# Attention beside a Fourier mixing layer on one core: the main loop's order of work from a written list instead of three round patterns

## The chip, the core and the metric

The kernel runs on one core of one Trainium2 chip. Its engines work side by side, each through its own queue in order: TensorE (PE, with its weight loads as PEld) multiplies, VectorE (DVE), ScalarE (ACT) and GpSimd (POOL) work on elements, and SyncE (SP) issues the DMA transfers. Matmul results go to PSUM, which has eight banks here named S0 to S5, F0 and V. The metric is the device time of one execution in microseconds: before the change 1810.23 us (median of three, 1810.04 to 1810.98).

## The reference

S is 2048, D 640, H 32 heads of width 20, one key and value head shared by all.

```python
g = sigmoid((x * gate_w).sum(-1, keepdims=True))
# Fourier mixing
a_ = einsum("bsd,ed->bse", x, dft_hid_re); b_ = einsum("bsd,ed->bse", x, dft_hid_im)
a = einsum("ts,bse->bte", dft_seq_re, a_) - einsum("ts,bse->bte", dft_seq_im, b_)
# attention, one k and v for 32 heads
q = x @ wq; k = x @ wk; v = x @ wv
p = softmax(q k^T * 20 ** -0.5); b = (p @ v) @ wo
out = g * a + (1 - g) * b
```

## The kernel before, in words

A first stage makes q, k and v, a second one the two products with the hidden DFT (tiles `ab`, line 125, with the first scores of head pair 0 among them). Then comes the main loop, 240 rounds, which this change rewrites; 16 rounds of another pattern (`ROUND_LAST`) for the last head pair; and the product with `wo`.

Three streams of matmuls are interleaved on PE in the main loop, by an order that the kernel writes out by hand (`manual_schedule`):

- **y**, the DFT along the sequence (line 645), done as seven block products. A y matmul has 64 rows: the contraction is halved between rows 0 to 63 (group 0, `y0`) and rows 64 to 127 (group 1, `y1`), and both halves add into the same bank F0. 96 y matmuls make one group of outputs, 48 groups fall in the main loop. The left operand is loaded and split in two by POOL (`load_c`, `split_c`, lines 450, 454, 455, tiles `craw`, `ch`, `cl`), in half blocks of 24 y matmuls per row group and with three buffers; the right operand by `split_x` (lines 482, 485, 486).
- **scores.** Two heads make a pair; head 0 has its queries and keys in rows 0 to 63, head 1 in rows 64 to 127. A score is computed twice. As `a` (line 330, queries by keys) it is read by DVE (line 337), which takes the row maximum; `a_reduce` and `a_final` turn a whole pair's maxima into two more rows of the queries' buffer, through DRAM. As `b` (line 750, keys by queries, with the maximum subtracted by those two rows) it is read by ACT (line 759), which writes the exponentials to one of 16 buffers `pt`. The a stream runs ahead of the b stream by a whole pair and `LEAD` = 12 units of a head. a and b share the six banks S0 to S5, so a score has to wait until the reader of its bank's previous score is done.
- **V**, the product of the exponentials with v (line 763, `av_step`): 128 rows by 32 columns, four column groups side by side, two passes of float32, so eight matmul instructions make one step.

A matmul of 64 rows in group 0 runs beside one in group 1. So the order pairs y of one row group with scores of the other, and changes sides: since both halves of y add into one bank, a y matmul that starts on a new side waits for the first reader (of an a or b) that was issued after the last y of the old side (`Halves.run`, `Halves.scored`). ROUND_10 and ROUND_9 are used in the ratio 3 to 2; in both a half round is y0 with the scores of rows 64 to 127, then a V, and the other half is y1 with the scores of rows 0 to 63, then a V. `c` is a `b` that takes the newest free `pt` buffer, `E` is the eviction of a finished y group by ACT.

The queries of a pair stand in one of three buffers; `load_qs` fills the next one by six DMAs on SP's queue when the a stream has done 17 units of a pair. `later(n, f)` runs `f` after n ticks, and a tick is every second `a` of the main loop. All loads of the main loop are issued from SP's one queue.

Of the kernel before, what the change touches and what calls it, by code (L numbers as in the profile page):

```python
# [10 lines left out]
AF = mybir.ActivationFunctionType  # L11
# [7 lines left out]
S = 2048  # L19
# [4 lines left out]
NT = S // P  # L24
NPAIR = H // 2
LAST = NPAIR - 1
# [8 lines left out]
def kernel(  # L35
# [274 lines left out]
    def load_qs(p):  # L310
        t = qbuf[p % 3]
        qs[p] = t
        for hh in range(2):
            r = slice((2 * p + hh) * DH, (2 * p + hh + 1) * DH)
            b = 64 * hh
            move(t[b : b + 20], qh_d[r])
            move(t[b + 20 : b + 40], qh_d[r])
            move(t[b + 40 : b + 60], ql_d[r])
# [47 lines left out]
    def later(n, f, *args):  # L366
        todo.append((clock["n"] + n, f, args))
# [6 lines left out]
            f(*args)  # L374

    NA = NPAIR * 64
    state = [0, 0]

    def a_half(hh, tag="A", main=False):
        u = state[hh]  # L380
        if u >= NA:
            return
        ins = a_unit(u, hh, tag)
        if main:
            halves.scored(ins)
        state[hh] = u + 1
        if state[1 - hh] <= u:
            return
        if u % 64 == 16 and u // 64 + 1 < NPAIR:
            load_qs(u // 64 + 1)  # L390
        if u % 64 == 63:
            later(1, a_reduce, u // 64)
            later(3, a_final, u // 64)


    cpools = [ctx.enter_context(tc.tile_pool(name="cp0", bufs=1))]
# [99 lines left out]

    load_qs(0)
    rot = Rot(["B", "F", "B", "F"])
    LEAD = 12
    done = 0  # L500
    for t in range(NT):
        load_x2(t + 2)
# [124 lines left out]
    class Halves:  # L627
# [3 lines left out]
            self.todo = [[], []]  # L631
            self.last = self.mark = None

        def put(self, ps2, w, x, start, stop):

            one = len(ps2) == 1
            for g, r in enumerate(RG):
                s0, s1 = start and not (one and g == 1), stop and not (one and g == 0)
                self.todo[g].append((ps2, w[r], x[r], s0, s1))

        def run(self, g):
            while not self.todo[g]:
                next(ys)
            ps, w, x, start, stop = self.todo[g].pop(0)
            mm = nc.tensor.matmul(ps[g % len(ps)], w, x, start=start, stop=stop)  # L645
            if len(ps) == 1:

                if not start and self.last != g:
                    tc.add_manual_dep(mm.ins, self.mark.ins.name, ORDER, reason="turns with a bank")
                self.last, self.mark = g, None  # L650

        def scored(self, ins):
            if self.mark is None:
                self.mark = ins

    ORDER = mybir.DependencyInfo(mybir.DependencyClass.Sync, mybir.DependencyReason.DATA)
    halves = Halves()
# [21 lines left out]
    def y_in(n, k):  # L679

        got = []
        for q, (_, old, _) in enumerate(PRODUCTS[n][2]):
            if old is not None:
                t = op.tile([P, HALF], F32, tag=f"ya{q}", name="ya")
                move(t, y_block(old, k))
                got.append(t)
        return got
# [15 lines left out]
    def f_stream():  # L703

        load_c(0, 1)
        split_c(0, 1)  # L710
        for g, (n, k) in enumerate(GROUPS):
            ps = [bank("F0", f"y_{n}_{k}")[:, :HALF]]
            if g >= GMAIN:
                ps.append(bank("S5", f"y_{n}_{k}_1")[:, :HALF])
            y0 = y_in(n, k)
            for sh in range(2):
                h, l = c_ops.pop((g, sh))
                load_c(g + 1, sh)
                for j in range(SJ):
                    if j == SJ // 2:  # L720
                        split_c(g + 1, sh)
                        if sh == 0:
                            load_x(n + 1, k)
                        else:
                            split_x(n + 1, k)
                    jj = sh * SJ + j
                    x = x_ops[n, jj // 2]
                    hi, lo = x[:, jj % 2], x[:, 2 + jj % 2]
                    last = jj == NT - 1
                    halves.put(ps, h[:, j], hi, jj == 0, False)  # L730
                    halves.put(ps, h[:, j], lo, False, False)
                    halves.put(ps, l[:, j], hi, False, last)
                    if last:
                        ended.append({"n": n, "k": k, "ps": ps, "y": y0})
                    yield

# [5 lines left out]

    ptfree = list(range(16))

    def b_unit(p, hh, kc, qc, tag, newest):
        b = 64 * hh
        ps = bank(tag, f"b_{p}_{kc}_{qc}_{hh}")
        nc.tensor.matmul(  # L750
            ps,
            ks[b : b + 62, kc * P : (kc + 1) * P],
            qs[p][b : b + 62, qc * ROW : (qc + 1) * ROW],
            start=True,
            stop=True,
        )
        slot = ptfree.pop(-1 if newest else 0)
        t = pp.tile([P, ROW], F32, tag=f"pt{slot}", name="pt")
        halves.scored(nc.scalar.activation(t, ps, AF.Exp, scale=SCALE))  # L759
        pt[(hh, kc, qc)] = t, slot  # L760

    def av_mm(ps, g, t, kc, first, last):
        nc.tensor.matmul(ps[32 * g : 32 * g + 32, :], vsb[:, kc, :], t, start=first, stop=last)  # L763

    def av_step(p, qh, kc):
        if kc == 0:
            av[qh] = bank("V", f"av_{p}_{qh}")
        for hh in range(2):
            for j in range(2):
                t, slot = pt.pop((hh, kc, 2 * qh + j))  # L770
                av_mm(av[qh], 2 * hh + j, t, kc, kc == 0, kc == NT - 1)
                ptfree.append(slot)

    def finish_half(p, qh):
        ob = op.tile([P, ROW], F32, name="ob")
        nc.scalar.activation(ob, av[qh], AF.Copy)
        for hh in range(2):
            h = 2 * p + hh
            for j in range(2):
                js = slice((2 * qh + j) * ROW, (2 * qh + j + 1) * ROW)  # L780
                g = 32 * (2 * hh + j)
                move(sum_d[h : h + 1, js], ob[g + DH : g + DH + 1])
                move(oT_d[h * DH : (h + 1) * DH, js], ob[g : g + DH])
        if p == LAST:
            sm = op.tile([P, 16], F32, name="sm")
            ts = slice(qh * S // 2, (qh + 1) * S // 2)
            for hh in range(2):
                move(sm[64 * hh : 64 * hh + 64], sum_d[2 * p + hh, ts].rearrange("(s t) -> s t", t=16))
            later(4, finish_last, ts, sm)
        elif qh == 1:  # L790
            sm = op.tile([P, 32], F32, name="sm")
            move(sm, sum_d[2 * p : 2 * p + 2].rearrange("h (s t) -> (h s) t", t=32))
            later(24, finish_sums, p, sm)
# [11 lines left out]
    def finish_last(ts, sm):  # L805
# [10 lines left out]

    ROUND_10 = (
        "a1S0 y0 b1S3 y0 y0 c1S1 y0 y0 a1S2 y0 a1S5 y0 y0 a1S4 y0 b1S0 c0S3 V a0S1 y1 y1 b0S0 "  # L820
        "y1 y1 a0S5 y1 a0S3 y1 y1 b0S2 y1 y1 a0S4 y1 c0S0 c1S1 V y0"
    ).split()
    ROUND_9 = (
        "a1S2 y0 b1S0 y0 y0 a1S1 y0 a1S5 y0 y0 a1S4 y0 y0 b1S3 y0 c0S2 c1S0 V a0S5 y1 b0S2 y1 "
        "y1 a0S1 y1 c0S0 y1 y1 a0S3 y1 y1 a0S4 y1 E0 b1S2 c0S5 V"
    ).split()

    ROUND_LAST = (
# [3 lines left out]
    ).split()  # L832
    ROUNDS = [(p, qh, kk) for p in range(NPAIR) for qh in range(2) for kk in range(NT // 2)]

    BEFORE = {
        4: (lambda: load_wo(range(3)), lambda: load_o(0), lambda: load_o(1)),
# [1 line left out]
        6: (lambda: split_o(0), lambda: load_o(2)),  # L838
        7: (lambda: [load_y(tb) for tb in range(4)],),
    }  # L840
    old = []
    for rnd in ROUNDS:
        p, qh, kk = rnd
        nb, na = [0, 0], 0
        turn = (p * NT + qh * SJ + kk) % 5
        new = [(p, qh, 2 * kk), (p, qh, 2 * kk + 1)]
        for what in ROUND_LAST if p == LAST else ROUND_10 if turn < 3 else ROUND_9:
            if what == "V":
                if old:
                    st = old.pop(0)  # L850
                    av_step(*st)
                    if st[2] == NT - 1:
                        finish_half(*st[:2])
                continue
            g = int(what[1])
            if what[0] == "y":
                halves.run(g)
            elif what[0] == "E":
                if p == LAST or turn == 4:
                    y_evict()  # L860
            elif what[0] in "bc":
                b_unit(p, g, 2 * kk + nb[g] // 2, 2 * qh + nb[g] % 2, what[2:], what[0] == "c")
                if p == LAST and sum(nb) % 2 == 0:
                    tick()
                nb[g] += 1
            else:
                if na % 2 == 0:
                    tick()
                a_half(g, what[2:], True)
                na += 1  # L870
        old += new
        if p == LAST and qh == 1:
            for f in BEFORE.get(kk, ()):
                f()
    for _ in range(2):
        y_evict()
    split_o(1)
# [69 lines left out]
```

## Time and profile before

| what | us |
|---|---|
| median of three runs | 1810.23 |
| profiled execution, first to last instruction | 1807.7 |
| PE busy | 1799.4 |
| DVE busy | 1457.3 |
| ACT busy | 1243.2 |
| POOL busy | 822.1 |
| granted TensorE clock | 1.000 |

The profiled execution's span is 2.5 us under the median. The stages by the trace: up to 89 us the projections, up to 248 us the hidden DFT, from 248 to 1626 us the main loop, to 1732 us the last pair's rounds, and then the output product. PE's busy share says that there is always a matmul under way, not that both row groups are: that is read from the starts of single matmuls.

### The profile page before, as it was taken

Reading aid. Unit: us, or ns where it says so; the run is one execution under the profiler, and the core shown is the slowest. Engines: PE = TensorE matmul, PEld = TensorE weight load, DVE = VectorE, ACT = ScalarE, POOL = GpSimd, SP = SyncE. Lnnn points to the kernel's source line nnn. Section 1 sums busy time; section 2 is a strip of 40 time slices with the busy share of each in tenths; the row PEclk is TensorE's granted clock in tenths of the full one; section 3 lists DMA queues with packets and bytes.
Section 4 is the critical chain, followed back from the end, with each engine's and each line's share of the span. In section 5 each row is a group of like instructions: output and inputs, shape, how many; then the busy total and the mean of one; then the engine's idle time right before and its main releaser. Section 6 shows DMA issues by size and latency. Waiting matters only on the chain.

```text
span 1807.7 us, 40911 instructions
## 1 busy us (share of the span) xinstructions
PE 1799.4 (100%) x16342; PEld 1215.1 (67%) x16342; DVE 1457.3 (81%) x2335; ACT 1243.2 (69%) x2327; POOL 822.1 (45%) x559
## 2 busy tenths in 40 slices
PE   9999999999999999999999999999999999999999
PEld 7799976666666666666666666666666666657789
DVE  4469988888888888888888888888888888853354
ACT  5432247777777777777777777777777777776731
POOL 1012136444546464666655565565554444342241
PEclk9999999999999999999999999999999999999999
DMA  8763334332344433444353434353433342315666
GB/s 267 227 192 99 115 100 139 116 108 84 130 125 133 121 119 106 153 126 152 112 167 101 156 112 141 113 153 115 136 112 114 87 126 79 97 59 169 207 215 209
DMA packets 131003, 243.89 MB, mean 135 GB/s; under 512 B 26356, under 2 KB 77556, under 8 KB 128292
## 3 DMA queue, kind: packets, MB, share of 16 engines
q1 hardware_dynamic: 130012, 238.00, 41.8%
q0 software_dynamic: 800, 3.28, 0.6%
q8 instruction: 128, 2.10, 0.5%
q14 instruction: 63, 0.52, 0.1%
HBM read 194.62 MB, written 50.86 MB: 136 GB/s over the span
## 4 chain that ended last, share of the span: by engine, by line
PE 99%; DMA 0%; POOL 0%; ACT 0%; DVE 0%; issue 0%; SPq 0%; ACTq 0%
PE av L763 28%; PE y L645 20%; PE a L330 18%; PE b L750 15%; PE ab L125 8%; PE q L114 1%; PE o L114 1%; PE q L115 1%; PE q L116 1%; PE o L116 1%; PE o L115 1%; PE kv L210 0%; PE kv L211 0%; DMA xr<-in_xT_dram 0%; DMA xr<-x_d 0%; ACT pt L759 0%
## 5 line engine op out<-in xcount | busy, mean ns | idle before, releaser
L337 DVE TENSOR_REDUCE mx<-a 128x1 f32<-128x512 f32 x2048 | 1291.3, 684 | 170.0 <-PE a L330 164.6
L759 ACT ACTIVATE pt<-b 128x512 f32<-128x512 f32 x2048 | 1110.7, 597 | 334.9 <-PE b L750 289.9
L645 PE MATMUL y<-x,ch 64*128 64x320 f32 x3584 | 796.6, 317 | 1.1 <-ACT pt L759 1.1
L330 PE MATMUL a<-ks,qs 60*128 60x512 f32 x2048 | 740.0, 416 | 0.0
L645 PEld LDWEIGHTS y<-x,ch 64*128 64x128 f32 x3584 | 552.3, 184 | 85.5 <-ACT pt L759 83.5
L750 PE MATMUL b<-qs,ks 62*128 62x512 f32 x2048 | 596.5, 405 | 0.6 <-DVE mx L337 0.6
L330 PEld LDWEIGHTS a<-ks,qs 60*128 60x128 f32 x2048 | 379.8, 185 | 277.0 <-ACT pt L759 197.4
L763 PE MATMUL av<-pt,vsb 128*32 128x512 f32 x4096 | 542.0, 604 | 0.0
L645 PE MATMUL y<-x,cl 64*128 64x320 f32 x1792 | 528.3, 311 | 0.5 <-POOL cl L455 0.5
L645 PEld LDWEIGHTS y<-x,cl 64*128 64x128 f32 x1792 | 314.7, 184 | 42.0 <-ACT pt L759 41.1
L750 PEld LDWEIGHTS b<-qs,ks 62*128 62x128 f32 x2048 | 314.0, 185 | 23.4 <-issue 6.7
L450 POOL TENSOR_TENSOR craw<-craw 128x1024 f32<-128x1024 f32 x80 | 191.1, 2388 | 236.2 <-DMA craw<-in_cre_dram 88.8
L455 POOL TENSOR_TENSOR cl<-craw,ch 128x1024 fp32r<-128x1024 f32 x98 | 234.2, 2389 | 7.9
L454 POOL CAST ch<-craw 128x1024 fp32r<-128x1024 f32 x98 | 101.7, 1038 | 182.2 <-PE y L645 153.4
L763 PEld LDWEIGHTS av<-pt,vsb 128*32 128x32 f32 x4096 | 82.3, 108 | 139.8 <-issue 131.5
L125 PE MATMUL ab<-wh,xh 64*128 64x320 f32 x640 | 136.0, 307 | 0.0
L125 PE MATMUL ab<-wl,xh 64*128 64x320 f32 x640 | 135.8, 306 | 0.0
L125 PE MATMUL ab<-wh,xl 64*128 64x320 f32 x640 | 135.6, 305 | 0.0
L698 POOL TENSOR_TENSOR ya<-yt,ya 128x320 f32<-128x320 f32 x64 | 59.4, 944 | 142.8 <-ACT yt L671 142.2
L524 ACT ACTIVATE half<-ab 128x320 f32<-128x320 f32 x64 | 28.0, 438 | 114.1 <-PE ab L125 100.8
L125 PEld LDWEIGHTS ab<-wh,xl 64*128 64x128 f32 x640 | 98.7, 184 | 0.0
L125 PEld LDWEIGHTS ab<-wl,xh 64*128 64x128 f32 x640 | 98.6, 185 | 0.0
(88 smaller groups left out, 1082.7 us busy)
## 6 DMA issues: line engine op xcount, KB each, us to landing
craw<-in_cre_dram SPq DMA_DIRECT2D x96, 512.0 KB
craw<-in_cim_dram SPq DMA_DIRECT2D x96, 512.0 KB
xr<-x_d SPq DMA_DIRECT2D x88, 320.0 KB
qs<-qh_d SPq DMA_DIRECT2D x64, 160.0 KB
x_d<-both SPq DMA_DIRECT2D x64, 160.0 KB
ya<-y_d SPq DMA_DIRECT2D x64, 160.0 KB
y_d<-ya SPq DMA_DIRECT2D x64, 160.0 KB
xr<-in_xT_dram SPq DMA_DIRECT2D x20, 256.0 KB
```

The lines of the kernel that those rows point to most:

```text
L114: nc.tensor.matmul(ps, wh, xh, start=(i == 0), stop=False)
L125: nc.tensor.matmul(ps, w[r], x[r], start=(i == 0 and k == 0), stop=(i == n - 1 and k == 2))
L330: nc.tensor.matmul(ps, qs[p][b : b + 60, qb * P : (qb + 1) * P], ks[b : b + 60, c * ROW : (c + 1) * ROW], start=True, stop=True,)
L337: return nc.vector.tensor_reduce(mx[p][:, hh, qb, c : c + 1], ps, axis=AX.X, op=ALU.max)
L450: eng.tensor_tensor(raw, raw, raws[1], op=PRODUCTS[n][0][1])
L454: eng.tensor_copy(h, raw)
L455: eng.tensor_tensor(l, raw, h.bitcast(F32), op=ALU.subtract)
L645: mm = nc.tensor.matmul(ps[g % len(ps)], w, x, start=start, stop=stop)
L698: nc.gpsimd.tensor_tensor(ya, yt, ya, op=how)
L750: nc.tensor.matmul(ps, ks[b : b + 62, kc * P : (kc + 1) * P], qs[p][b : b + 62, qc * ROW : (qc + 1) * ROW], start=True, stop=True,)
L759: halves.scored(nc.scalar.activation(t, ps, AF.Exp, scale=SCALE))
L763: nc.tensor.matmul(ps[32 * g : 32 * g + 32, :], vsb[:, kc, :], t, start=first, stop=last)
```

## The change

The two patterns ROUND_10 and ROUND_9 go. In their place stands a list of 8942 letters (`PLAN`) for all 240 rounds, one letter for each piece of work: `0` and `1` are a y matmul of row group 0 or 1, `V` a step with v, `-` an eviction of a y group, and the 24 letters of `SCORES` a score: `a` to `f` and `A` to `F` an `a` of head 0 or 1, `g` to `l` and `G` to `L` a `b` of head 0 or 1, the letter's place naming its bank S0 to S5. The list holds 2304 each of `0` and `1`, 944 `a` and 960 `b` for each head, 478 `V` and 48 `-`. Beside that:

- `put` no longer fixes which y matmul starts or stops a bank: `run` counts them (`grp`), so that either side can begin.
- The `pt` buffer of a `b` is chosen by `pick`: the newest of those whose last reader is known to be done from waits made before; `known`, `last` and `waits` keep that account while the program is built.
- `LEAD` is 16 instead of 12, so eight more `a` fall into the second stage.
- `load_qs` of the next pair is called only when both heads have issued all `b` that use its buffer (`need`, `ready`).
- `a_final` comes two ticks after a pair's last `a` instead of three.
- The last pair's 16 rounds keep their pattern; a step with v still comes two steps behind its scores (`LAG`).

```diff
+    taken = {"b": [0, 0], "a": 0, "V": 0}
+    need = []
+    def ready():
+        while need and min(taken["b"]) >= 64 * (need[0] - 2):
+            load_qs(need.pop(0))
...
-            load_qs(u // 64 + 1)
+            need.append(u // 64 + 1)
+            ready()
         if u % 64 == 63:
             later(1, a_reduce, u // 64)
-            later(3, a_final, u // 64)
+            later(2, a_final, u // 64)
...
-    LEAD = 12
+    LEAD = 16
...
+            one = len(ps) == 1
+            k = 0 if one else g
+            start, stop = grp[k] == 0, grp[k] == (6 if one else 3) * NT - 1
+            grp[k] += 1
             mm = nc.tensor.matmul(ps[g % len(ps)], w, x, start=start, stop=stop)
...
+    def pick(own):
+        lim = max(own, known["ACT"])
+        fit = [s for s in ptfree if s[0] <= lim]
+        best = max(fit or ptfree)
+        known["ACT"] = max(known["ACT"], best[0]) if not fit else known["ACT"]
+        ptfree.remove(best)
+        return best[1]
...
-    ROUND_10 = (
-        "a1S0 y0 b1S3 y0 y0 c1S1 y0 y0 a1S2 y0 a1S5 y0 y0 a1S4 y0 b1S0 c0S3 V a0S1 y1 y1 b0S0 "
-        "y1 y1 a0S5 y1 a0S3 y1 y1 b0S2 y1 y1 a0S4 y1 c0S0 c1S1 V y0"
-    ).split()
...
+    SCORES = "abcdefABCDEFghijklGHIJKL"
+    PLAN = (
+        "gBId1K11l1a111h1c11j11k11f11ah11i11j11eFVHa0E0I000F00J0H000A0C00K0DL00H0A00K0VCd0L0A0hEV1i1lDh11aVeI"
+        "0L0D00A0H000I0K00F0D00H00A0C000F000K0BjVVa11k1c11j11f1h11a1k11c11j1h11f11e1g1-VVJcHfGe1VJc1h11f1g111"
...
+    for what in PLAN:
+        if what == "V":
+            next_v()
+        elif what == "-":
+            y_evict()
+            known["y"] = taken["b"][0] + taken["b"][1] - 1
+        elif what in "01":
+            halves.run(int(what))
+        else:
+            kind, s = divmod(SCORES.index(what), 6)
+            if kind >= 2:
+                if min(state) >= NA and sum(taken["b"]) % 2 == 0:
+                    tick()
+                next_b(kind - 2, f"S{s}")
+            else:
+                if taken["a"] % 2 == 0:
+                    tick()
+                waits(f"S{s}", -1)
+                a_half(kind, f"S{s}", True)
+                taken["a"] += 1
```

More of the change, by code (lines that the diff above doesn't have):

```diff
@@ L632, in __init__, with put @@
             self.last = self.mark = None
-        def put(self, ps2, w, x, start, stop):
-            one = len(ps2) == 1
+        def put(self, ps2, w, x, grp):
             for g, r in enumerate(RG):
-                s0, s1 = start and not (one and g == 1), stop and not (one and g == 0)
-                self.todo[g].append((ps2, w[r], x[r], s0, s1))
+                self.todo[g].append((ps2, w[r], x[r], grp))
         def run(self, g):
@@ L643, in run, with scored @@
                 next(ys)
-            ps, w, x, start, stop = self.todo[g].pop(0)
+            ps, w, x, grp = self.todo[g].pop(0)
+            one = len(ps) == 1
+            k = 0 if one else g
+            start, stop = grp[k] == 0, grp[k] == (6 if one else 3) * NT - 1
+            grp[k] += 1
             mm = nc.tensor.matmul(ps[g % len(ps)], w, x, start=start, stop=stop)
-            if len(ps) == 1:
+            if one:
                 if not start and self.last != g:
                     tc.add_manual_dep(mm.ins, self.mark.ins.name, ORDER, reason="turns with a bank")
+                    known["PE"] = max(known["PE"], self.exp)
+                if start:
+                    known["PE"] = max(known["PE"], known["y"])
                 self.last, self.mark = g, None
-        def scored(self, ins):
+        def scored(self, ins, n=-1):
             if self.mark is None:
-                self.mark = ins
+                self.mark, self.exp = ins, n
     ORDER = mybir.DependencyInfo(mybir.DependencyClass.Sync, mybir.DependencyReason.DATA)
@@ L715, in f_stream @@
             y0 = y_in(n, k)
+            grp = [0, 0]
             for sh in range(2):
@@ L728, in f_stream @@
                     hi, lo = x[:, jj % 2], x[:, 2 + jj % 2]
[L729 to L733, printed above, removed]
+                    halves.put(ps, h[:, j], hi, grp)
+                    halves.put(ps, h[:, j], lo, grp)
+                    halves.put(ps, l[:, j], hi, grp)
+                    if jj == NT - 1:
                         ended.append({"n": n, "k": k, "ps": ps, "y": y0})
@@ L741, with waits, b_unit @@
     pt = {}
-    ptfree = list(range(16))
-    def b_unit(p, hh, kc, qc, tag, newest):
+    ptfree = [(-1, k) for k in range(16)]
+    known = {"PE": -1, "ACT": -1, "y": -1}
+    last = {}
+    def waits(tag, n):
+        own = last.get(tag, -1)
+        last[tag] = n
+        if own <= known["PE"]:
+            return -1
+        known["PE"] = own
+        return own
+    def pick(own):
[5 more added lines that the diff above has]
+        return best[1]
+    def b_unit(p, hh, kc, qc, tag):
         b = 64 * hh
@@ L756, in b_unit @@
         )
-        slot = ptfree.pop(-1 if newest else 0)
+        n = taken["b"][0] + taken["b"][1]
+        slot = pick(waits(tag, n))
         t = pp.tile([P, ROW], F32, tag=f"pt{slot}", name="pt")
-        halves.scored(nc.scalar.activation(t, ps, AF.Exp, scale=SCALE))
-        pt[(hh, kc, qc)] = t, slot
+        halves.scored(nc.scalar.activation(t, ps, AF.Exp, scale=SCALE), n)
+        pt[(hh, kc, qc)] = t, (n, slot)
     def av_mm(ps, g, t, kc, first, last):
@@ L770, in av_step @@
                 t, slot = pt.pop((hh, kc, 2 * qh + j))
+                known["PE"] = max(known["PE"], slot[0])
                 av_mm(av[qh], 2 * hh + j, t, kc, kc == 0, kc == NT - 1)
@@ L812, in finish_last @@
             move(rx_d[h * DH : (h + 1) * DH, ts], rec_d[h : h + 1, ts].to_broadcast([DH, S // 2]))
-    ROUND_10 = (
-        "a1S0 y0 b1S3 y0 y0 c1S1 y0 y0 a1S2 y0 a1S5 y0 y0 a1S4 y0 b1S0 c0S3 V a0S1 y1 y1 b0S0 "
-        "y1 y1 a0S5 y1 a0S3 y1 y1 b0S2 y1 y1 a0S4 y1 c0S0 c1S1 V y0"
-    ).split()
[L823 to L826, printed above, removed]
+    SCORES = "abcdefABCDEFghijklGHIJKL"
@@ L832 @@
     ).split()
-    ROUNDS = [(p, qh, kk) for p in range(NPAIR) for qh in range(2) for kk in range(NT // 2)]
+    STEPS = [(p, qh, kc) for p in range(NPAIR) for qh in range(2) for kc in range(NT)]
     BEFORE = {
@@ L840 @@
     }
[L841 to L847, printed above, removed]
-            if what == "V":
[L849 to L857, printed above, removed]
-            elif what[0] == "E":
[L859 to L863, printed above, removed]
-                    tick()
[L865 to L874, printed above, removed]
@@ new lines, with next_b, next_v @@
+    LAG = 2
+    taken["V"] = LAG
+    def next_b(g, tag):
+        r, nb = divmod(taken["b"][g], 4)
+        p, qh, kc = STEPS[2 * r + nb // 2]
+        b_unit(p, g, kc, 2 * qh + nb % 2, tag)
+        taken["b"][g] += 1
+        ready()
+    def next_v():
+        st = taken["V"] - LAG
+        taken["V"] += 1
+        if st >= 0:
+            av_step(*STEPS[st])
+            if STEPS[st][2] == NT - 1:
+                finish_half(*STEPS[st][:2])
+    for what in PLAN:
[18 more added lines that the diff above has]
+                taken["a"] += 1
@@ L875 @@
+    for kk in range(NT):
+        for what in ROUND_LAST:
+            if what == "V":
+                next_v()
+            elif what[0] == "E":
+                y_evict()
+            elif what[0] == "y":
+                halves.run(int(what[1]))
+            else:
+                if sum(taken["b"]) % 2 == 0:
+                    tick()
+                next_b(int(what[1]), what[2:])
+        for f in BEFORE.get(kk - NT // 2, ()):
+            f()
+    old = STEPS[-LAG:]
     for _ in range(2):
```

89 lines of the change are left out of this document (added).

## The prediction

> **What bounds the kernel now.** I read the page's table of engines and its chain first, then the groups by line, then PE's timeline inside one period of the main loop.
>
> ```profile
> PE 1799.4 (100%) x16342; PEld 1215.1 (67%) x16342; DVE 1457.3 (81%) x2335; ACT 1243.2 (69%) x2327; POOL 822.1 (45%) x559
> PE 99%; DMA 0%; POOL 0%; ACT 0%; DVE 0%; issue 0%; SPq 0%; ACTq 0%
> L337 DVE TENSOR_REDUCE mx<-a 128x1 f32<-128x512 f32 x2048 | 1291.3, 684 | 170.0 <-PE a L330 164.6
> L759 ACT ACTIVATE pt<-b 128x512 f32<-128x512 f32 x2048 | 1110.7, 597 | 334.9 <-PE b L750 289.9
> L763 PE MATMUL av<-pt,vsb 128*32 128x512 f32 x4096 | 542.0, 604 | 0.0
> 800.00:1000.00 200.00, 200.00 (x1792) 122.22 (x1792) 176.22 (x286) 155.95 (x292) 114.51 (x77) 1.00 0.44 138
> ```
>
> The chain is PE for 99% of the span, and the two readers of the scores wait for PE (164.6 and 289.9 us). The last row is the window from 800 to 1000 us, busy times of PE, weight loads, DVE, ACT and POOL: the clock is full at 1.00, DVE stands at 88%, ACT at 78%, POOL at 57%. So PE sets the end, with DVE next. What PE spends, its timeline shows:
>
> ```profile
> 256.01 1.06 PE L763 MATMUL av<-pt,vsb 128*32 128x512 f32 x8
> ...
> 896.63 1.06 PE L763 MATMUL av<-pt,vsb 128*32 128x512 f32 x8
> 897.63 0.41 PE L645 MATMUL y<-x,cl 64*128 64x320 f32 x1
> ...
> 897.88 0.31 PE L645 MATMUL y<-x,ch 64*128 64x320 f32 x1
> 897.97 0.39 PE L750 MATMUL b<-qs,ks 62*128 62x512 f32 x1
> 898.03 0.31 PE L645 MATMUL y<-x,ch 64*128 64x320 f32 x1
> 898.18 0.30 PE L645 MATMUL y<-x,cl 64*128 64x320 f32 x1
> 898.20 0.39 PE L330 MATMUL a<-ks,qs 60*128 60x512 f32 x1
> 898.32 0.30 PE L645 MATMUL y<-x,ch 64*128 64x320 f32 x1
> 898.43 0.39 PE L330 MATMUL a<-ks,qs 60*128 60x512 f32 x1
> 898.46 0.30 PE L645 MATMUL y<-x,ch 64*128 64x320 f32 x1
> 898.61 0.31 PE L645 MATMUL y<-x,cl 64*128 64x320 f32 x1
> 898.66 0.40 PE L330 MATMUL a<-ks,qs 60*128 60x512 f32 x1
> 898.76 0.45 PE L645 MATMUL y<-x,ch 64*128 64x320 f32 x2
> ...
> 899.05 0.31 PE L645 MATMUL y<-x,cl 64*128 64x320 f32 x1
> 899.14 0.44 PE L750 MATMUL b<-qs,ks 62*128 62x512 f32 x2
> 899.51 1.07 PE L763 MATMUL av<-pt,vsb 128*32 128x512 f32 x8
> ...
> 1624.72 1.07 PE L763 MATMUL av<-pt,vsb 128*32 128x512 f32 x8
> 1626.21 0.38 PE L645 MATMUL y<-x,ch 64*128 64x320 f32 x1 [0.43 <-ACT pt L759]
> ...
> 1630.74 1.92 PE L763 MATMUL av<-pt,vsb 128*32 128x512 f32 x16
> 1632.59 0.50 PE L750 MATMUL b<-qs,ks 62*128 62x512 f32 x2
> ```
>
> Durations overlap, so I price by starts. Within one row group a y follows a y after 0.146 us (897.88 to 899.05 in eight steps, one of them inside the merged row at 898.76) and a score a score after 0.23 (898.20, .43, .66); the two groups run beside each other. A block of one V keeps everything else off for 1.00 us (896.63 to 897.63), a block of two, which only the last pair's rounds have, for 1.85 (1630.74 to 1632.59): a step itself is 0.85. Round a block there is more: the last b's start at 899.14, V only at 899.51; and the y at 897.63 is followed by the next of its group after 0.25, not 0.146.
>
> I take this loss per block from the whole loop. From the first block (256.01) to the last (1624.72) are 477 periods, 1368.7 us, **2.869 us** each. A stretch between blocks costs its fuller row group: with ten y and one score 10 x 0.146 + 0.23 = 1.69 us, and where there are nine y the side with seven scores, 1.61. Six of the one and four of the other in five rounds make 1.658. So a block loses 2.869 - 1.658 - 0.85 = **0.36 us** beyond the steps in it.
>
> **The change part by part.** *Fewer blocks.* Both loops hold 478 steps. The patterns put every one in a block of its own: 478. In the list I count 294 runs of V, taking V on either side of a `-` together, since that letter is ACT's: 113 single, 178 double, 3 triple. So 184 blocks go, at 0.36 each: **-66.4 us**.
>
> *Stretches.* The same sum of fuller sides, over the old 478 stretches, is 795.8 us; over the list's it is 809.7: 83 stretches hold just six scores, three on each side, no y (0.69 us each); 158 hold twelve scores or more (4.17 us on average); and the sides are less even. **+13.9 us**, price by price the same rows.
>
> *LEAD.* Eight scores a move into the second stage, beside its matmuls, where one costs half of 0.23 with the other row group filled: **+0.9**. Their absence from the list is in the sum above.
>
> *Waits for banks.* The trace of before shows hardly any, so this one is bounded. A stretch brings scores one after another at 0.23 us, a and b mixed, and their readers are slower:
>
> ```profile
> 899.83 1.08 ACT L759 ACTIVATE pt<-b 128x512 f32<-128x512 f32 x2
> 903.89 2.48 DVE L337 TENSOR_REDUCE mx<-a 128x1 f32<-128x512 f32 x4 [0.36 <-PE a L330]
> ```
>
> Four reductions take 2.48, the last of them 0.684: 0.60 from start to start. Two exponentials take 1.08: 0.49. Two scores come in 0.46, so DVE falls 0.14 behind with each a. In the old stretches of eight scores that is four reductions, 2.4 us in a period of 2.87. The list's 158 long stretches hold 8.8 a and 9.2 b on average. What DVE has not read at the end of a stretch it reads in the block after it; what exceeds the banks stops PE. If a stretch may leave four of its reductions for later (four of the six banks hold an a), the excess of 0.60 x (a - 4) over the stretch's PE time, summed over the list, is 0; if three, 2.3 us; if two, 42.1 us. Taking two as the worst split, the bounds are 0 and 42; nothing here can be gained. The six banks are dealt to a and b in all three ways, so I take the mean of the three values: **+15 us**. ACT's like sums (0.49, b for a) are under 6 and lie in the same time.
>
> *At no cost, with their cover.* The queries' held loads:
>
> ```profile
> SPq L106 <- PE b L750: 38.3, 11, 6.2
> ```
>
> SP now stands 38.3 us in eleven waits for the last b on a buffer, with the other loads queued behind; held back, these shrink. PE never waited for those loads, so nothing is gained; the load is due only 47 a units of a head later, 66 us at 1.4 us a unit (1322 / 944). The two rows of maxima have less room:
>
> ```profile
> 874.89 0.29 DVE L343 TENSOR_REDUCE mxr<-mx 128x32 f32<-128x128 f32 x1
> 878.46 0.32 SPq L106 DMA_DIRECT2D m_d<-ms  x1
> 879.95 2.51 SPq L106 DMA_DIRECT2D qs<-m_d  x4
> 892.20 0.39 PE L750 MATMUL b<-qs,ks 62*128 62x512 f32 x1
> ```
>
> From the pair's reduction to the last of the four issues pass 7.6 us, and the pair's first b comes 17.3 after the reduction. In the list the slower head has 8 to 17 units in hand when a pair's first b comes, at least 11 us; `a_final` one tick earlier returns 1.4. That holds; were the cover gone, it would be a few us at a pair. y changes sides 98 times in the list instead of 479. The new side waits for a reader issued after the old side's last y, and the block of V between hides it; the row at 1626.21 is such a wait left uncovered, 0.43 us, which would be 42 us for all 98. ACT's copy of a finished V bank falls between blocks as before, and the flags counted in `run` and the choice of `pt` buffers add no instruction of an engine.
>
> The sum: 1807.7 - 66.4 + 13.9 + 0.9 + 15 = 1771.1 us of span; the median of the runs stands 2.5 higher, so **1773.6**.
>
> **The rivals.** *The readers become the bound.* With the worst split, waits of 42.1 give 1807.7 - 66.4 + 13.9 + 0.9 + 42.1 + 2.5 = **1800.7**. For it: DVE needs 1888 x 0.60 = 1133 us of a loop of about 1322 (809.7 + 478 x 0.85 + 294 x 0.36), in bursts. Against: it is idle in every period now (0.36 before the four at 903.89). The page "TensorEngine Tiling (Array Packing)" of the Trainium skill, section Performance Considerations, says the same as a rule: tiling speeds up TensorE but not the reading of PSUM, which may become the bottleneck. In this trace the readers still wait for PE. This mechanism ends on the **other side** when the waits pass 66.4 - 14.8 = 51.6 us: at 0.63 us a reduction and two left over, the sum over the list is 62.0, so **1820.6**; at 0.684, no overlap between reductions, 113.9 and 1872.
>
> *y is fed too late.* The list lets one row group run up to 27 y ahead of the other, where it was 10, and a side can go through the end of one half block and into the next, 3.5 us apart at these prices:
>
> ```profile
> 265.16 2.39 POOL L450 TENSOR_TENSOR craw<-craw 128x1024 f32<-128x1024 f32 x1 [3.37 <-DMA craw<-in_cre_dram]
> 274.52 2.39 POOL L450 TENSOR_TENSOR craw<-craw 128x1024 f32<-128x1024 f32 x1 [3.39 <-DMA craw<-in_cre_dram]
> L645 PE MATMUL y<-x,cl 64*128 64x320 f32 x1792 | 528.3, 311 | 0.5 <-POOL cl L455 0.5
> ```
>
> A load-bound half block takes POOL 9.4 us; y waited 0.5 us in all. Against: the buffer that a half block needs is free at least 17 us of PE work before the second of two close ones, so 7.6 us remain. If POOL came one half block behind, 9.4 - 7.6 = 1.8 us over 47 groups is 84.6, and **1858**; it turns the sign from 36.6 / 47 = 0.8 us a group.
>
> *The steps are not really merged*: the second V of a block waits for its exponentials, or for ACT's copy of the bank where a head pair's half ends, and each of the 184 keeps its 0.36: 1807.7 + 13.9 + 0.9 + 15 + 2.5 = **1840**. For it: PE has waited for ACT 0.43 us at 1626.21. Against: the block of sixteen at 1630.74 ran through in 1.85.
>
> *Nothing is lost*: the sides' unevenness is filled across a block's edge and no bank is late, 1807.7 - 66.4 + 0.9 + 2.5 = **1744.7**.
>
> **How the numbers follow.** A measurement of this kernel can tell a change from none at about 0.2%, 3.6 us. Forecast (waits up to 30 us, 1759 to 1788): 0.63. Readers bound but still faster (1788 to 1806): 0.14; within 3.6 us of before, by the same waits: 0.04; beyond, slower: 0.04. Late y: 0.03. Not merged: 0.04. Nothing lost (1745 to 1758): 0.08. Faster 0.63 + 0.14 + 0.08 = 0.85, same 0.04, slower 0.11. From 1750 to 1802 lie the forecast, most of the readers' case and half of the last: 0.63 + 0.11 + 0.05, about 0.8.
>
> **What would show it.** Right: some 311 blocks of V by the timeline (294 and the last rounds' 17), double ones of 1.85 us; the last block of the main loop about 37 us earlier than 1624.72; DVE at 90% between 800 and 1000 us. Waits of PE for DVE or ACT before a or b, several times the old ones, show the readers' term; sums beyond 50 us, or POOL cl before y, would make the forecast wrong.

## The result, and the profile after

| kernel | median us | runs | span of the profiled execution |
|---|---|---|---|
| before | 1810.47 (1810.04 to 1810.98) | 4 | 1807.7 |
| after | 1780.39 (1779.9 to 1782.14) | 4 | 1778.5 |

The ratio is 0.9839, 95% interval 0.9825 to 0.9853: 30.1 us faster, where 36.6 were forecast (1773.6). It lies inside the stated range and inside the forecast's own case, 1759 to 1788.

The page of the kernel after, in the same places as before: the table of engines, the chain, the groups of the two readers, of the scores' weight loads and of the step with v (its line is now 799, that of y 656, of b 785, of the exponential 795), and last the window from 800 to 1000 us.

```profile
PE 1771.3 (100%) x16342; PEld 1267.5 (71%) x16342; DVE 1426.2 (80%) x2335; ACT 1187.1 (67%) x2327; POOL 821.9 (46%) x559
PE 99%; DMA 0%; ACT 0%; DVE 0%; SPq 0%; issue 0%; ACTq 0%
L337 DVE TENSOR_REDUCE mx<-a 128x1 f32<-128x512 f32 x2048 | 1265.6, 683 | 171.4 <-PE a L330 118.6
L795 ACT ACTIVATE pt<-b 128x512 f32<-128x512 f32 x2048 | 1053.6, 619 | 338.7 <-PE b L785 200.4
L330 PEld LDWEIGHTS a<-ks,qs 60*128 60x128 f32 x2048 | 350.6, 185 | 135.6 <-DVE mx L337 100.1
L785 PEld LDWEIGHTS b<-qs,ks 62*128 62x128 f32 x2048 | 345.9, 185 | 122.4 <-ACT pt L795 61.8
L656 PE MATMUL y<-x,cl 64*128 64x320 f32 x1792 | 522.8, 308 | 0.0
L799 PE MATMUL av<-pt,vsb 128*32 128x512 f32 x4096 | 504.2, 600 | 0.0
800.00:1000.00 200.00, 200.00 (x1822) 132.86 (x1819) 175.53 (x292) 151.02 (x298) 124.91 (x83) 1.00 0.46 145
```

The counts of instructions are the same, PE is the chain as before, and y waits for POOL nowhere (0.0 in the row of `cl`; that the other row group does not hide such a wait there is read from the starts below). In the same 200 us PE runs 1822 matmuls instead of 1792. DVE is busy 175.53 us, hardly other than the 176.22 of before, though it makes 292 instructions in place of 286. Its instructions overlap more, so its busy time stands still while its work grows; it did not reach the 90% that the prediction named.

PE's timeline, the first block of V and the block that holds the 477th and the 478th step:

```profile
253.77 0.64 PE L799 MATMUL av<-pt,vsb 128*32 128x512 f32 x4
...
1593.44 1.92 PE L799 MATMUL av<-pt,vsb 128*32 128x512 f32 x16
1595.30 0.41 PE L656 MATMUL y<-x,ch 64*128 64x320 f32 x1
```

Before, these points stood at 256.01 and 1624.72. The stretch from the first block to the last is 1339.67 us after and 1368.71 before: **29.0 us** of the 29.2 that the two spans differ by lie in the main loop, between these two points. Ahead of the first block another 2.2 us are gained, and about as much is lost behind the last. (The first row is cut by the window to the last four of the block's eight matmuls that still ran; its time is the block's start.)

Over the whole trace there are 311 blocks: 113 of one step, 178 of two and 3 of three in the main loop, and the 17 of the last rounds. The double ones take 1.85 us, as the last rows show (1593.44 to 1595.30).

The loop's time divides into blocks and stretches between them. A stretch runs from the first matmul after a block to the next block's start; its price is its fuller row group, at 0.146 us a y and 0.23 a score, as in the prediction.

| us | before | after |
|---|---|---|
| blocks | 476.5 (478) | 451.0 (294) |
| stretches | 893.7 (477) | 890.5 (293) |
| of these, price | 790.8 | 805.6 |
| of these, beyond the price | 102.9, 0.216 each | 84.9, 0.290 each |

So the blocks gave 25.5 us. The stretches' price rose by 14.8. The price is a count over the list at the old rates, not a measurement. Beyond the price the old loop lost 0.216 us a stretch, nearly all of its stretches between 0.19 and 0.25; at that rate 293 stretches lose 63.3, and the list's lose **21.6 us more**. Sorted by the number of scores in a stretch, the loss beyond the price is

| scores in the stretch | stretches | mean loss after, us | half readers (below) |
|---|---|---|---|
| 4 to 7, no y | 83 | 0.213 | 0.208 |
| 4 to 7, with y | 13 | 0.211 | 0.206 |
| 8 to 11 | 40 | 0.249 | 0.214 |
| 12 to 15 | 60 | 0.285 | 0.214 |
| 16 to 19 | 62 | 0.340 | 0.218 |
| 20 to 23 | 10 | 0.371 | 0.218 |
| 24 to 28 | 25 | 0.506 | 0.229 |

Short stretches lose what the old ones did, and the loss grows with the length. One of the longest, 26 scores and 37 y, in the timeline of PE and then of DVE and ACT:

```profile
1275.03 0.50 PE L330 MATMUL a<-ks,qs 60*128 60x512 f32 x1
...
1276.60 0.39 PE L330 MATMUL a<-ks,qs 60*128 60x512 f32 x1
...
1277.12 0.50 PE L330 MATMUL a<-ks,qs 60*128 60x512 f32 x1
...
1277.71 0.50 PE L330 MATMUL a<-ks,qs 60*128 60x512 f32 x1
1277.82 0.31 PE L656 MATMUL y<-x,cl 64*128 64x320 f32 x1
1277.97 0.31 PE L656 MATMUL y<-x,ch 64*128 64x320 f32 x1
1278.05 0.40 PE L785 MATMUL b<-qs,ks 62*128 62x512 f32 x1
1278.12 0.31 PE L656 MATMUL y<-x,ch 64*128 64x320 f32 x1
1278.31 0.49 PE L785 MATMUL b<-qs,ks 62*128 62x512 f32 x1
...
1281.73 1.06 PE L799 MATMUL av<-pt,vsb 128*32 128x512 f32 x8
```

```profile
1276.44 7.20 DVE L337 TENSOR_REDUCE mx<-a 128x1 f32<-128x512 f32 x12
```

```profile
1275.61 6.72 ACT L795 ACTIVATE pt<-b 128x512 f32<-128x512 f32 x13 [1.72 <-PE a L330]
```

The stretch lasts 6.70 us (1275.03 to 1281.73) against a price of 5.86. Both readers run without a pause, DVE twelve reductions in 7.20 us from 1276.44 on, ACT thirteen exponentials in 6.72 from 1275.61 on. A score that follows its side's last one without a wait has a record of about 0.39 us, as at 1276.60; those at 1277.12, 1277.71 and 1278.31 have 0.49 or 0.50. The same 0.50 stands at the first score after a block (1275.03). Over the whole trace the weight load of a score with a short record starts 0.22 us ahead of its matmul (the median), that of a score with a long record starts with it: the weights were not loaded ahead. PE never stands idle in such a stretch, the y go on, and so the rows of waits do not show this loss. Those of the scores' weight loads even fall, from 300.4 us in the two rows before to the 258.0 of the two above:

```profile
L330 PEld LDWEIGHTS a<-ks,qs 60*128 60x128 f32 x2048 | 379.8, 185 | 277.0 <-ACT pt L759 197.4
L750 PEld LDWEIGHTS b<-qs,ks 62*128 62x128 f32 x2048 | 314.0, 185 | 23.4 <-issue 6.7
```

The loss is seen only by adding up the starts. The starts also say that y is not late: of 4325 y that directly follow one of their own row group in a stretch, six come more than 0.26 us after it.

### The profile page after: what moved, and what is told of

Same layout as the page of the kernel before. It is cut to its first block, busy times and chain, and to the rows that moved or that the text cites. A ratio compares the mean times of both kernels' runs of the same rounds, so it can differ in the third digit from the quotient of the medians.

```text
span 1778.5 us, 40725 instructions
## 1 busy us (share of the span) xinstructions
PE 1771.3 (100%) x16342; PEld 1267.5 (71%) x16342; DVE 1426.2 (80%) x2335; ACT 1187.1 (67%) x2327; POOL 821.9 (46%) x559
## 4 chain that ended last, share of the span: by engine, by line
PE 99%; DMA 0%; ACT 0%; DVE 0%; SPq 0%; issue 0%; ACTq 0%
PE av L799 27%; PE y L656 21%; PE a L330 17%; PE b L785 17%; PE ab L125 8%; PE o L114 1%; PE q L114 1%; PE q L116 1%; PE o L116 1%; PE o L115 1%; PE q L115 1%; DMA wqraw<-in_wq_dram 0%; PE kv L211 0%; PE kv L210 0%; PE kvt L231 0%; DVE wql L110 0%
## 5 line engine op out<-in xcount | busy, mean ns | idle before, releaser
L337 DVE TENSOR_REDUCE mx<-a 128x1 f32<-128x512 f32 x2048 | 1265.6, 683 | 171.4 <-PE a L330 118.6
L795 ACT ACTIVATE pt<-b 128x512 f32<-128x512 f32 x2048 | 1053.6, 619 | 338.7 <-PE b L785 200.4
L656 PE MATMUL y<-x,ch 64*128 64x320 f32 x3584 | 757.5, 309 | 0.3 <-ACT yt L685 0.3
L785 PE MATMUL b<-qs,ks 62*128 62x512 f32 x2048 | 720.7, 424 | 0.0
L656 PEld LDWEIGHTS y<-x,ch 64*128 64x128 f32 x3584 | 564.4, 185 | 27.4 <-issue 15.9
L799 PE MATMUL av<-pt,vsb 128*32 128x512 f32 x4096 | 504.2, 600 | 0.0
L330 PEld LDWEIGHTS a<-ks,qs 60*128 60x128 f32 x2048 | 350.6, 185 | 135.6 <-DVE mx L337 100.1
L785 PEld LDWEIGHTS b<-qs,ks 62*128 62x128 f32 x2048 | 345.9, 185 | 122.4 <-ACT pt L795 61.8
L799 PEld LDWEIGHTS av<-pt,vsb 128*32 128x32 f32 x4096 | 107.5, 108 | 197.6 <-issue 176.3
L125 PEld LDWEIGHTS ab<-wh,xl 64*128 64x128 f32 x640 | 91.8, 184 | 0.0
```

The lines of the kernel that those rows point to most:

```text
L125: nc.tensor.matmul(ps, w[r], x[r], start=(i == 0 and k == 0), stop=(i == n - 1 and k == 2))
L330: nc.tensor.matmul(ps, qs[p][b : b + 60, qb * P : (qb + 1) * P], ks[b : b + 60, c * ROW : (c + 1) * ROW], start=True, stop=True,)
L337: return nc.vector.tensor_reduce(mx[p][:, hh, qb, c : c + 1], ps, axis=AX.X, op=ALU.max)
L785: nc.tensor.matmul(ps, ks[b : b + 62, kc * P : (kc + 1) * P], qs[p][b : b + 62, qc * ROW : (qc + 1) * ROW], start=True, stop=True,)
```

## The experiments

### Taking the merged blocks apart

The list unchanged, but the second V of a block comes six letters later:

```diff
+    def apart(plan, n=6):
+        out, held, seen = [], 0, 0
+        for c in plan:
+            if c == "V" and (held or "".join(out[-2:]).rstrip("-")[-1:] == "V"):
+                held += 1
+                continue
+            out.append(c)
+            if held and c not in "V-":
+                seen += 1
+                if seen == n:
+                    out.append("V")
+                    held, seen = held - 1, 0
+        return out + ["V"] * held
-    for what in PLAN:
+    for what in apart(PLAN):
```

> The list as it is, but a block of several V is taken apart: its second V comes six letters (y or scores) later, so nearly every step is a block of its own again, 478 of them instead of 294. If a block costs 0.36 us beyond its steps, the 184 new blocks cost 66 us, and the less even stretches 20 us more (830.6 instead of 810.9 us by the starts' prices): about 1866 us. If blocks are worth nothing and the gain came from elsewhere in the list: 1780 to 1800 us.

Measured: 1870.9 us (one run), 90.5 over the list's kernel and 61.8 over the kernel before. The trace has 478 blocks of one step in the main loop again. Taking off the 20 us of less even stretches, 70.8 us remain for 184 blocks, 0.38 each, beside 0.36 from the old period. The trace divides them: against the list's loop the blocks take 29.2 us more, and the stretches lose 42.1 us more beyond their price. So a block costs this much beyond its steps in an order that is otherwise the new one; the list with single blocks would be worse than the old patterns. What the array does in this time no run here takes apart.

### Merging alone, on the old patterns

```diff
             if what == "V":
-                if old:
...
+                nv += 1
+                for _ in range(1 if p == LAST else 0 if nv == 1 else 2):
+                    if old:
...
```

> The two old round patterns, with the first V of each round moved behind the round's second one: 239 blocks of two, nothing else changed. Merging alone, without the list, would give 239 x 0.36 = 86 us and 11 us of stretches: about 1713 us. If the change of y's side needs a block of V in front of it to hide the wait for a reader, the 239 changes in the middle of a round are now bare: at least 0.43 us each (the one bare wait of the trace of before) and up to a reader's queue of 1 us, and six banks must carry sixteen scores between blocks; then 1815 to 1960 us.

Measured: 1968.46 us (one run), 159 slower than before, somewhat beyond the upper end of the second theory. The main loop has 239 blocks of two, all of 1.85 us, so the blocks are merged. The saving was lost again, with 159 us on top: the loop's 238 stretches now lose 1.28 us each beyond their price instead of 0.216, 253 us in all, in changes of side and, with sixteen scores between two blocks, in waits for banks; the two were not taken apart. A change in PE's timeline, in the middle of a round:

```profile
903.28 0.31 PE L645 MATMUL y<-x,ch 64*128 64x320 f32 x1
903.37 0.47 PE L750 MATMUL b<-qs,ks 62*128 62x512 f32 x2
903.84 0.49 PE L330 MATMUL a<-ks,qs 60*128 60x512 f32 x1
904.46 0.41 PE L645 MATMUL y<-x,cl 64*128 64x320 f32 x1
904.47 0.50 PE L750 MATMUL b<-qs,ks 62*128 62x512 f32 x1
```

and the waits of the whole run:

```profile
PEld y L645 <- ACT pt L759: 210.6, 385, 1.2
```

The last y of one side starts at 903.28 and the first of the other at 904.46, 1.18 us later; the change waits for a reader issued after the old side's last y, and it is ACT. Over 235 such changes it is 1.35 us on average, room enough for the whole loss, though a bank that came free late can be part of it. (Before, the same row of waits had 124.6 us in 149 times, behind blocks of V.) In the old order the block of V stands in this place. Merging therefore needs another cover for a change of side. The list has it: only 98 changes, each of them with a block of V between the old side's last y and the new side's first, and 83 stretches of six scores between two blocks, where no y runs at all.

### Faster readers under the list

First a maximum over 256 of 512 columns, then the exponential too (the other half of each buffer holds ones), then the exponential alone. These parts of the computation are left out.

```diff
...
-        return nc.vector.tensor_reduce(mx[p][:, hh, qb, c : c + 1], ps, axis=AX.X, op=ALU.max)
+        return nc.vector.tensor_reduce(mx[p][:, hh, qb, c : c + 1], ps[:, : ROW // 2], axis=AX.X, op=ALU.max)
...
-        halves.scored(nc.scalar.activation(t, ps, AF.Exp, scale=SCALE), n)
+        halves.scored(nc.scalar.activation(t[:, : ROW // 2], ps[:, : ROW // 2], AF.Exp, scale=SCALE), n)
```

> The list's kernel with the row maximum taken over the first 256 of a score's 512 columns only (this part of the computation is left out), so a reduction holds its bank and DVE for about 0.33 us in place of 0.60. If the 21.6 us that the long stretches lose beyond the fixed 0.216 us of a stretch are waits for banks that DVE holds, 10 to 20 us are gained: 1760 to 1770 us. If they are ACT's or no waits at all, under 4 us: 1776 to 1780 us.

> As the half reduction, and the exponential too is taken over 256 of the 512 columns only (the other half of each buffer holds ones, written once before the main loop). If the long stretches' loss is waits for readers of either kind, it goes nearly all: 1757 to 1766 us. If it lies in the matmuls' own pace, nothing changes by more than 4 us: 1776 to 1780 us.

> The list's kernel with only the exponential over 256 of 512 columns (the rest of each buffer holds ones); the maximum is whole. The half maximum alone gained 5.4 us, both halves 22.4. If ACT's exponentials hold the banks that most late scores wait for: 1762 to 1768 us. If either reader keeps the six banks late while the other is quick: 1772 to 1776 us, and the two single gains together stay well under 22.

| kernel | median us | ratio to before, 95% interval | gain on the list's 1780.39 | beyond the price, 293 stretches |
|---|---|---|---|---|
| half maximum | 1775.01 | 0.9807 (0.9791 to 0.9823) | 5.4 | 78.8 |
| half exponential | 1773.53 | 0.9804 (0.9789 to 0.9818) | 6.9 | 78.6 |
| both | 1757.95 | 0.9715 (0.9701 to 0.973) | 22.4 | 62.8 |

With both readers quick the stretches lose 62.8 us, 0.214 each, and the last column of the table above is flat: a stretch of 26 scores loses hardly more than one of six. The rest, 84.9 - 62.8 = **22.1 us**, is the waits for the readers, and it is the whole gain. That they are waits for banks, and not of V for its exponentials, shows at the stretches' ends: from the last score to the block it is 0.36 us on average, with and without the cut. The long stretch shown above, with the same 26 scores and 37 y, starts and ends here at

```profile
1259.64 0.50 PE L330 MATMUL a<-ks,qs 60*128 60x512 f32 x1
...
1261.37 0.39 PE L788 MATMUL b<-qs,ks 62*128 62x512 f32 x1
...
1265.76 1.07 PE L802 MATMUL av<-pt,vsb 128*32 128x512 f32 x8
```

6.12 us instead of 6.70. The readers' groups of this run:

```profile
L337 DVE TENSOR_REDUCE mx<-a 128x1 f32<-128x256 f32 x2048 | 800.1, 421 | 605.5 <-PE a L330 358.9 <-PE b L788 165.2 <-PE y L659 62.3
L798 ACT ACTIVATE pt<-b 128x256 f32<-128x256 f32 x2048 | 707.3, 384 | 641.9 <-PE b L788 363.2 <-PE a L330 186.3 <-PE y L659 58.9
```

A reduction is down from 683 to 421 ns and an exponential from 619 to 384. Of the single cuts, the half maximum fell between the bounds of the two theories: 5.4 us lies above the 4 of the one and below the 10 of the other. The half exponential answers why, by its second theory: 5.4 and 6.9 make 12.3, not 22.4. Either reader alone is late enough to hold up the order; with one of them quick, PE waits more often for the other's banks. The list names each score's bank, and so the reader that had to empty it; counted are the scores with a record over 0.46 us, which had to wait, without those that come first on their side after a block:

| long records among the scores in the stretches | bank last read by DVE (1618 scores) | by ACT (1636 scores) |
|---|---|---|
| list | 309 | 137 |
| half maximum | 25 | 209 |
| half exponential | 424 | 37 |
| both | 29 | 47 |

### The control: faster readers before

> The control: the kernel before, with maximum and exponential over 256 of 512 columns (that part is left out, the other half of each buffer holds ones). If the 22 us that the same cut gained under the list were waits for banks that only the list's long stretches have, nothing changes here: 1806 to 1813 us. If faster readers help any order of this loop, some 20 us go here too: about 1790 us.

The same cut of both readers on the kernel before: 1804.04 us, ratio 0.9972 (0.9962 to 0.9982), 5.5 us faster than the 1809.55 beside it. That is 2 us outside the 1806 to 1813 expected for no change, and a quarter of what the list gained. In its loop a stretch loses 0.209 instead of 0.216, 3.3 us over 477; another 1.2 us lies ahead of the loop, whose first y starts at 247.0 instead of 248.2. So the old loop had 3 us of such waits too, and the list's loop has 22.

### Everything but the list

```diff
...
-            load_qs(u // 64 + 1)
+            need.append(u // 64 + 1)
+            ready()
...
-            later(3, a_final, u // 64)
+            later(2, a_final, u // 64)
...
-    LEAD = 12
+    LEAD = 16
...
```

> Everything of the change but the list, on the old round patterns: LEAD 16, the queries' loads held until both heads are done with the buffer, a_final after two ticks. If these cost and bring nothing, as predicted: 1806 to 1813 us. If the held loads free SP's queue for something that PE waits for, or the eight a in the second stage cost more than they save: beyond 3.6 us of before on the one or the other side.

Measured: 1810.73 us, ratio 1.0007 (0.9998 to 1.0017). These parts bring and cost nothing that can be measured. Under the list the held loads do what was said of them, and SP's waits show it, in the kernel after:

```profile
SPq L106 <- PE b L785: 12.2, 4, 5.1
```

38.3 us in eleven waits became 12.2 in four. On the old patterns, with the same held loads, these waits are longer instead, 99.0 us in sixteen, and the time does not change there.

## Why the prediction was right, and where its sum was off

- *PE sets the end, and a block of V costs 0.36 us beyond its steps.* Right: taken apart again, the blocks cost 0.38 each, and the stretches' fixed loss and the blocks' time fell in proportion to the 184 that went.
- *The list's stretches are less even, 13.9 us.* Right. The 14.8 of the table is the same count between the first block and the last, and so no test of it; the test is the half readers, which leave the price, 0.21 us a stretch at every length, and nothing else.
- *Waits for banks, +15.* Right in kind, too small: 22.1 by the half readers, 21.6 by the table. This is the mis-sized term. It failed in two steps. The sum took DVE's excess and said that ACT's "lie in the same time"; the half maximum took nearly all of DVE's away and left 16 of the 22. So ACT's were not covered by DVE's, and where both are slow more is lost than either makes alone. And the mean over three splits of the banks is a guess between 0 and 42, not a count; that the half exponential leaves 15.8 us, near the 15 that were worked out for DVE, is luck. The other terms, -66.4 + 13.9 + 0.9 = -51.6, meet what is measured: 29.2 + 21.6 = 50.8.
- *LEAD, the held loads and a_final at no cost.* Right together: 1.0007. The 0.9 us put down for LEAD is too small to be seen. That held loads shrink SP's waits holds under the list, not by itself.
- *The rivals.* The readers are the bound in the longest stretches, where both run through without a pause, but not in the loop: 22 us of waits, not the 51.6 from which they would have made it slower. The Trainium skill says that tiling speeds up TensorE but not the reading of PSUM, which may become the bottleneck ("TensorEngine Tiling (Array Packing)", Performance Considerations). For that part the trace agrees: with half the reading the kernel is 22.4 us faster. y came late nowhere: its row of `cl` shows no wait, and six of 4325 starts in a row group are late. The steps are merged: 1.85 us a double block. That nothing is lost would have been 1744.7; with half readers the kernel takes 1757.95, and the 13.3 between them are the unevenness, which no reader fills.
- *What would show it.* 311 blocks and 1.85 us were right. The loop's last block came 31 us earlier, not 37: the loop itself gave 29.0, short by the waits, and 2.2 lie ahead of its first block. DVE's share did not rise to 90%. And the sign given for the readers' term was wrong: waits of PE for DVE or ACT ahead of a score do not grow several times over; the two rows of the scores' weight loads fall, while the y of the other side keep PE busy.

## What to carry to other kernels

A switch between two ways of using PE's array has a price of its own, here 0.36 us, that no row of busy time shows; it comes out of the period, less the work of the fuller side and of the step itself, and it is saved by gathering what needs the other way. Before gathering, look for what the switch was hiding: here it covered the change of y's side, and merging without a new cover cost 159 us. Where two engines read from shared banks, price both together, and test with both made quick: one alone showed a quarter to a third of what the two were worth.

## What was not expected

The waits for banks are almost invisible: PE is 100% busy and the y run on, while the scores' side loses 0.1 to 0.3 us in each stretch of twelve scores or more. Besides the wait itself, a score that waited has a record of 0.49 or 0.50 us in place of 0.39, as the first one after a block has: its weight load, which otherwise runs 0.22 us ahead, starts with it.

Whether another list could win back part of the 22 us of waits without more blocks was not tried.
